# Keys contracted with x instead of with values, and wv applied to the result, in a linear-attention and gated-MLP kernel

## The chip, the core and the metric

The kernel runs on one NeuronCore of a Trainium2 chip. The core has five engines that work side by side, each with its own in-order queue: TensorE (PE, matrix products; loading of the stationary operand is shown as PEld), VectorE (DVE), ScalarE (ACT), GpSimd (POOL) and SyncE (SP, which here only issues DMA transfers). They meet in SBUF, the on-chip memory of 128 partitions, and in the PSUM banks into which TensorE accumulates. The metric is the time in microseconds from the first to the last instruction of one execution, lower is better; a run's time is measured without a profile, and one further execution is profiled.

## What is computed

With S = 2048 rows, D = 1024 columns, H = 32 heads of 32 and F = 3584, all in float32:

```python
def phi(t): return where(t > 0, t + 1, exp(t)) + 1e-6
xn = layernorm(x)
q, k, v = split(xn @ wqkv)                       # each [H, S, 32]
pq, pk = phi(q), phi(k)
kv = einsum("hsd,hse->hde", pk, v)               # 32 x 32 per head, over all rows
z  = einsum("hsd->hd", pk)
o  = einsum("hqd,hde->hqe", pq, kv) / (einsum("hqd,hd->hq", pq, z) + 1e-6)
s  = o @ wo
g  = silu((silu(xn @ w1) * (xn @ w3)) @ w2)
out = x + s * g
```

The attention has no softmax over pairs of rows: keys and values meet only in `kv`, a sum over all rows. Since v = xn wv, the same sum can be taken as kv = wv' (xn' pk), with ' for the transpose, one block of heads at a time.

## The kernel before

**Products.** Float32 operands are split by `split` (L84) into a high part (an ACT copy to the reduced type fp32r) and a low part (a DVE subtraction), and `mm3` (L93) adds three products: high by high, high by low, low by high. All large products are done with seven block products in place of eight, by sums of blocks (the names A11, S1 to S4 on the side of x, B11, T1 to T4 on the side of the weights). `gemm` (L400) is one such product: 256 output columns for 1024 rows, 7 x 4 x 3 = 84 instructions of 512 columns. Its results come as four tiles (n, c): n is the block of 128 output columns, c the block of 512 rows; `use(n, c, tile)` is called on each as it is complete.

**Two halves.** `half(h)` (L525) handles 1024 rows. In half 0, x is loaded, normalised, turned and combined by `prepare_first` and `prepare_rest` (L167, L191), where POOL makes the sums of untransposed blocks (L202 to L205). The first four gemms of half 0 are `early`: they begin on A11 and A12 while the sums are still being made. Then come the keys and values of the four pairs (a pair is 256 columns), the queries (4 gemms) and the two hidden layers (28 gemms). For half 1, `prepare_next` (L211) makes the same operands during half 0 and keeps them in DRAM (`a_d`), from which half 1 loads them at its beginning.

**Keys and values.** `keys_values` (L484) keeps phi(k) of a pair (`pk`), then takes the values; each of the four blocks is turned, key and value, into rows by TensorE transposes against an identity and an ACT eviction (`to_rows`, L477), and a kv step (L509) contracts the rows over 512 tokens, 4 x [128 x 128 x 128] in plain float32, and adds them to `kvacc` in SBUF (L515). These steps are put into `later`.

**What fills the gaps.** `catch_up` (L388) is called six times in an ordinary gemm. It takes one entry of `later`, or else one step of the current job: `next_work` in half 0 (the operands of half 1, then sums of w2 blocks), `attention_work` in half 1 (`spread_z`, denominators, `merge_wo`, which multiplies kv into wo, and `divide`, which scales the queries). Jobs load two ahead into three `job` buffers. What is left over at the end of a half is emitted after its last gemm (L594).

**Buffers and queues.** The `raw` tag has two buffers of 1 MB: x at the beginning, then each weight pair (`Operands.ask`, L297), later the merged wo. The `b` tag of pool `pb` has eight buffers for split operands. SP issues loads in order and waits at each for its buffer; POOL issues most stores in order among its own arithmetic. A planner orders each engine's queue ahead of the run, by readiness in its own model of time and by the order in the program.

Of the kernel before, what the change touches and what calls it, by code (L numbers as in the profile page):

```python
# [22 lines left out]
def tile_linear_attention_times_swiglu(  # L23
# [85 lines left out]
    kvacc = st.tile([P, ND, P], F32, tag="kvacc", bufs=1, name="kvacc")  # L109
    nc.vector.memset(kvacc, 0.0)  # L110

    def small(name):
        return pc.tile([P, C], F32, tag="c", name=name)
# [50 lines left out]
    def operand_tiles(h):  # L164
        return {n: pa.tile([P, 2, ND // 2, C], FR, tag=n, name=f"{n}_{h}") for n in AOPS}

    def prepare_first(A, mom):  # L167

        xs = []
        for g in range(TH // 4):  # L170
            t = load_rows([(2 * g + e) * P for e in range(2)], f"xa{g}")
            xs += [t[:, e] for e in range(2)]
            for i in (2 * g, 2 * g + 1):
                moments(xs[i:i + 1], mom[:, i:i + 1])
                normalise(xs[i], mom[:, i])
                turn_into(A, {"A11": xs[i][:, :C]}, i, f"0_{i}")
# [14 lines left out]
    def prepare_rest(A, mom, i, t0, seconds, behind):  # L191

        with ExitStack() as order:
            for mark in behind:
                order.enter_context(tc.issue_after(mark.ins))
            if i % 2 == 0:
                seconds += load_second(mom, i // 2)
            t1, s1 = seconds[i], small(f"S1x{i}")
            normalise(t1, mom[:, TH // 2 + i])

            a11, a12, a21, a22 = t0[:, :C], t0[:, C:], t1[:, :C], t1[:, C:]
            nc.gpsimd.tensor_add(out=s1, in0=a21, in1=a22)  # L202
            nc.gpsimd.tensor_sub(out=a21, in0=a11, in1=a21)
            nc.gpsimd.tensor_sub(out=a11, in0=s1, in1=a11)
            last = nc.gpsimd.tensor_sub(out=a12, in0=a12, in1=a11)  # L205
        behind.append(last)
        yield
        turned, _ = turn_into(A, {"S2": a11, "S3": a21, "S1": s1, "A22": a22, "S4": a12}, i, f"0_{i}")
        yield turned

    def prepare_next(i):  # L211
# [8 lines left out]
        def steps(_):  # L220
# [22 lines left out]
                yield True  # L243

            a11, a12, a21, a22 = (t[c][:, n * C:(n + 1) * C] for c in range(2) for n in range(2))
            p_ = turn("A11", a11)
            keep("A11", p_)
            nc.scalar.copy(out=a11, in_=p_)
# [232 lines left out]
            nc.tensor.transpose(p_[:, t * P:(t + 1) * P], src[:, t * P:(t + 1) * P], ident)  # L481
        nc.scalar.activation(dst, p_.rearrange("p (t d) -> p t d", t=C // P), AF.Identity, bias=bias)

    def keys_values(h, pair):  # L484

        pk, todo, rows = {}, [], {}

        def use_k(n, c, src):
            j = 2 * pair + n
            pk[n, c] = signed(f"pk{h}_{j}_{c}")  # L490
            z = st.tile([P, 1], F32, tag="z", name="z")
            phi(src, pk[n, c], z)
# [3 lines left out]
        def use_v(n, c, src):  # L496
            if (n, c) == (0, 0):
                v = small(f"v{h}_{pair}")
                nc.scalar.copy(out=v, in_=src)
                src = v  # L500
            todo.append((n, c, src))

        def turn(n, c, v):
            name = f"{h}_{2 * pair + n}_{c}"
            rows[n, c] = pb.tile([P, 2, C // P, P], F32, tag="b", name=f"kvr{name}")
            to_rows(rows[n, c][:, 0], pk[n, c], f"k{name}", 1e-6)
            to_rows(rows[n, c][:, 1], v, f"v{name}")

        def kv(n, c):  # L509
            j = 2 * pair + n  # L510
            r = rows[n, c]
            acc = bank(f"kv{h}_{j}_{c}")[:, :P]
            for t in range(C // P):
                nc.tensor.matmul(acc, lhsT=r[:, 1, t], rhs=r[:, 0, t], start=t == 0, stop=t == C // P - 1)  # L514
            nc.vector.tensor_add(out=kvacc[:, j], in0=acc, in1=kvacc[:, j])  # L515

        def step(i):
            if i:
                kv(*todo[i - 1][:2])
            if i < len(todo):  # L520
                turn(*todo[i])

        return use_k, use_v, [lambda i=i: step(i) for i in range(5)]

    def half(h):  # L525
        A = operand_tiles(h)

        def keys(pair, **how):
            return gemm(ops[f"k{h}_{pair}_"], A, uses[pair][0], **how)

        def values(pair, **how):
            return gemm(ops[f"v{h}_{pair}_"], A, uses[pair][1], **how)

        def run(g):
            for _ in g:
                pass
# [2 lines left out]
            for _ in zip_longest(*gemms):  # L539
                pass  # L540

        uses = [keys_values(h, pair) for pair in range(ND // 2)]
# [23 lines left out]
        for pair in range(ND // 2):  # L566
            if h == 0 and pair < 2:
                run(m[2 * pair])
                run(m[2 * pair + 1])
            elif h and pair == 0:  # L570
                side_by_side(keys(pair, paired=True), values(pair, paired=True))
            else:
                run(keys(pair))
                run(values(pair))
            later.extend(uses[pair][2])
        jobs.append((attention_work(), False) if h else (next_work(), True))
        for pair in range(ND // 2):

# [161 lines left out]
    def divide(m, k):  # L740
# [25 lines left out]

        return Job(load, steps)

    def merge_wo(k):

        both = []
# [7 lines left out]
        def steps(e, t):  # L779
            both.append(t)  # L780
            j = k + e * (ND // 2)
            f = small(f"kvf{j}")[:, :P]
            nc.vector.tensor_mul(f, hmask, kvacc[:, j])
            kvm = st.tile([P, 2, P], FR, tag="kvm", bufs=1, name=f"kvm{j}")
            split(kvm, f)
# [41 lines left out]

    groups = []
    for h in range(NH):
        some = [Operands(wqkv, part * D + pair * 2 * P, f"{'qkv'[part]}{h}_{pair}_", h == 0 and part and pair < 2,  # L830
                         h and part == 2 and pair == 0)
                for parts in ((1, 2), (0,)) for pair in range(ND // 2) for part in parts]
# [6 lines left out]
    for o, o.next in zip(ops, ops[1:]):  # L839
        pass  # L840
    ops = {o.name: o for o in ops}
    stages = in_turn(groups)
    for h in range(NH):
        half(h)
    jobs.append((late_work(), True))
# [300 lines left out]
```

## Time and profile before

| | |
|---|---|
| median of three runs | 2376.68 us (2375.96 to 2380.29) |
| span of the profiled execution | 2378.6 us |
| DMA | 416.77 MB, 175 GB/s on average |
| float32 kv contractions | 128 (256 records) |
| transposes of key rows | 128 |
| transposes of value rows | 128 |

The page of a profile gives each engine's busy time and its share of the span, the same in 40 slices of 59.5 us (a digit is a tenth), and groups of instructions with their count, busy time, mean duration and the idle time before them with what ended it ("<-"). A row of a timeline gives start, duration, engine, line, operation and operands ("out<-in"), and in brackets the idle time before it. Durations of neighbouring products overlap, since the array is pipelined: the price of one is the distance between starts. In a list of waits stand the waiting engine and tile, who ended the wait, and the us in total, the count and the longest.

### The profile page before, as it was taken

To read this page: it belongs to the slowest core of one execution; us is meant where nothing else is said; L and a number is where in the kernel's file an instruction comes from. 1 tells how busy PE (TensorE), PEld (TensorE's weight loads), DVE (VectorE), ACT (ScalarE), POOL (GpSimd) and SP (SyncE) were. 2 spreads that over 40 slices of the span, in tenths; PEclk is the share of its full clock that TensorE was granted. 3 is DMA by queue.
4 is the path that set the end of the run, shared out by engine and by line. 5 is a ranking of instruction groups with operands and counts; after the bars stand their busy time and mean duration, and the time that the engine had idled before them with its cause. 6 is when DMAs were issued, how large, how long until landed. Compare 5 with 4: busy or idle time off the path is not lost.

```text
span 2378.6 us, 30952 instructions
## 1 busy us (share of the span) xinstructions
PE 2330.0 (98%) x10624; PEld 1920.7 (81%) x10624; DVE 1752.6 (74%) x2810; ACT 912.6 (38%) x1621; POOL 637.5 (27%) x752
## 2 busy tenths in 40 slices
PE   6999999999999999999999999999999999999998
PEld 5788888778888888877888887788787788888877
DVE  8755888888887665657788877787755676767698
ACT  4434554342333234434443232324323543343433
POOL 3000122438786420001343434242321000000033
PEclk9999999999999999999999999999999999999999
DMA  3211454567666671125546556464776665766588
GB/s 124 89 53 54 142 169 155 177 184 234 197 221 203 200 280 53 54 76 169 166 158 212 180 173 200 153 191 156 258 230 196 192 205 158 237 194 193 181 277 265
DMA packets 319903, 416.77 MB, mean 175 GB/s; under 512 B 21265, under 2 KB 251665, under 8 KB 319633
## 3 DMA queue, kind: packets, MB, share of 16 engines
q1 hardware_dynamic: 291712, 327.74, 43.6%
q0 software_dynamic: 28032, 87.06, 11.3%
q8 instruction: 83, 1.36, 0.2%
q14 instruction: 76, 0.61, 0.1%
HBM read 277.35 MB, written 141.03 MB: 176 GB/s over the span
## 4 chain that ended last, share of the span: by engine, by line
PE 51%; DMA 4%; issue 4%; DVE 3%; POOL 1%; ACT 1%; SPq 0%; POOLq 0%; DVEq 0%; ACTq 0%
PE cB L96 1%; PE dB L98 1%; PE cB L98 1%; PE dB L96 1%; PE dB L97 1%; PE cB L97 1%; PE aB L98 1%; PE aB L97 1%; PE aB L96 1%; PE bB L98 1%; PE bB L97 1%; PE bB L96 1%; PE kv L514 1%; DVE acc L896 1%; DMA rA22B<-h_d 1%
## 5 line engine op out<-in xcount | busy, mean ns | idle before, releaser
L625 POOL DMA_DIRECT2D h_d<-sg x112 | 82.8, 740 | 334.3 <-DVE sg L621 318.6
L583 POOL DMA_DIRECT2D pq_d<-pq x32 | 17.5, 548 | 469.2 <-DVE pq L475 454.4
L913 POOL DMA_DIRECT2D u_d<-uB x32 | 17.3, 542 | 407.1 <-DVE uB L896 393.0
L896 DVE TENSOR_TENSOR acc<-cB,acc 128x512 f32<-128x512 f32 x50 | 34.4, 687 | 40.6 <-PE cB L98 40.6
L896 DVE TENSOR_TENSOR acc<-dB,acc 128x512 f32<-128x512 f32 x56 | 38.5, 688 | 31.0 <-PE dB L98 31.0
L607 POOL TENSOR_TENSOR hs<-sg 128x256 f32<-128x256 f32 x56 | 60.9, 1087 | 0.0
L605 POOL TENSOR_TENSOR hs<-hs,sg 128x256 f32<-128x256 f32 x56 | 59.9, 1069 | 0.0
L608 POOL TENSOR_TENSOR hs<-sg,hs 128x256 f32<-128x256 f32 x56 | 58.0, 1036 | 1.5
L762 POOL DMA_DIRECT2D qs_d<-qd x32 | 18.0, 561 | 138.8 <-DVE qd L758 138.6
L604 POOL TENSOR_TENSOR hs<-sg,sg 128x256 f32<-128x256 f32 x56 | 49.7, 887 | 1.2
L633 POOL DMA_DIRECT2D h_d<-hs x60 | 46.0, 767 | 4.5 <-POOL hs L608 2.7
L640 POOL TENSOR_TENSOR w<-w 128x256 f32<-128x256 f32 x28 | 26.8, 957 | 55.2 <-DMA w<-in_B_w 47.8
L88 ACT CAST XS4B<-rS4B 128x384 fp32r<-128x384 f32 (+1 forms) x40 | 19.7, 493 | 57.0 <-PE cB L98 40.7
L1027 POOL DMA_DIRECT2D s_d<-s x32 | 17.5, 546 | 87.4 <-DVE s L896 42.4
L763 POOL DMA_DIRECT2D qs_d<-qd x32 | 27.0, 844 | 37.6 <-DVE qd L608 21.7
L88 ACT CAST XA22B<-rA22B 128x384 fp32r<-128x384 f32 (+1 forms) x40 | 19.7, 493 | 44.2 <-PE aB L98 26.4
L88 ACT CAST XA11B<-rA11B 128x384 fp32r<-128x384 f32 (+1 forms) x40 | 19.7, 493 | 43.6 <-PE dB L98 26.8
L96 PE MATMUL cB<-T,XS3B 128*128 128x512 f32 x87 | 34.4, 395 | 2.0 <-ACT XS3B L88 2.0
L88 ACT CAST XS3B<-rS3B 128x384 fp32r<-128x384 f32 (+1 forms) x40 | 19.7, 492 | 43.1 <-PE bB L98 20.4
L96 PE MATMUL aB<-B,XA11B 128*128 128x512 f32 x87 | 34.3, 395 | 1.4 <-ACT XA11B L88 1.4
L514 PEld LDWEIGHTS kv<-kvr 128*128 128x128 f32 x256 | 33.5, 191 | 2.5
L88 ACT CAST XA12B<-rA12B 128x384 fp32r<-128x384 f32 (+1 forms) x40 | 19.7, 494 | 41.0 <-PE dB L98 24.3
(5845 smaller groups left out, 8612.6 us busy)
## 6 DMA issues: line engine op xcount, KB each, us to landing
h_d<-hs POOLq DMA_DIRECT2D x60, 256.0 KB, 3.1
h_d<-sg POOLq DMA_DIRECT2D x56, 256.0 KB, 3.3
w<-in_B_w SPq DMA_DIRECT2D x56, 256.0 KB
wt_d<-w SPq DMA_DIRECT2D x28, 512.0 KB
h_d<-hs SPq DMA_DIRECT2D x52, 256.0 KB
qs_d<-qd POOLq DMA_DIRECT2D x32, 384.0 KB, 3.8
pq_d<-pq POOLq DMA_DIRECT2D x32, 256.0 KB, 3.3
a_dS<-xo SPq DMA_DIRECT2D x16, 512.0 KB
```

The costliest lines, as they stand in the source:

```text
L88: nc.scalar.copy(out=hi, in_=src)
L96: nc.tensor.matmul(acc, lhsT=wh, rhs=ah, start=start, stop=False, skip_group_check=True)
L97: nc.tensor.matmul(acc, lhsT=wh, rhs=al, start=False, stop=False, skip_group_check=True)
L98: nc.tensor.matmul(acc, lhsT=wl, rhs=ah, start=False, stop=stop, skip_group_check=True)
L514: nc.tensor.matmul(acc, lhsT=r[:, 1, t], rhs=r[:, 0, t], start=t == 0, stop=t == C // P - 1)
L604: e.tensor_add(out=s1, in0=a21, in1=a22)
L605: e.tensor_sub(out=s2, in0=s1, in1=a11)
L607: e.tensor_sub(out=s3, in0=a11, in1=a21)
L608: e.tensor_sub(out=s4, in0=a12, in1=s2)
L625: nc.gpsimd.dma_start(out=h_d[i][2 * h + c][:, 2 * n:4 * n + 2, k], in_=src)
L633: queue.dma_start(out=h_d[i][2 * h + c][:, 6 + 4 * e:10 + 4 * e, k], in_=o[e].rearrange("p (e s) -> p e s", s=P))
L896: return V.tensor_add(out=c, in0=src, in1=c)
```

## The change

The value gemms, the turning of the values, the kv steps and `kvacc` are gone. In their place:

- The normalised rows of x and the seven sums of their blocks are stored to DRAM (`x_d`), in half 0 from `prepare_first` and `prepare_rest`, in half 1 from `prepare_next`, all from POOL's queue. `prepare_next` makes four more POOL sums for it per block of rows.
- The key rows, and the sums of them that the seven products need, are stored to `y_d`, also from POOL's queue. All four early gemms of half 0 are now keys.
- After the keys of half 1, `row_products` runs seven products over all rows: each has four steps (two halves, two steps in each; a step is two token blocks of 128 and 24 matrix products), which load x rows and key rows from DRAM through the two `raw` buffers, split them, and accumulate x' pk into four banks. The seventh also loads a block that POOL subtracts. `row_sums` combines the results into `g_d`.
- In half 1's jobs, `key_values(j)` loads the columns of x' pk of block j and the columns of wv, contracts them in float32 (eight products of 128 x 128 x 128 for each of eight blocks), masks the result by head and hands it to `merge_wo`.
- The list of weight operands loses the value parts, and the query operands of half 1 are asked for near the end of `row_products`.

```diff
+    XS = ["A11", "A12", "S1", "S3", "A22", "S2", "S4"]
+    YS = ["Y00", "Y01", "Y10", "R5", "R2", "R4"]
+    x_d = [dram.tile([P, TH // 2, len(XS), C], F32, name=f"x_d{h}") for h in range(NH)]
+    y_d = [dram.tile([P, TH // 2, len(YS), ND // 2, P], F32, name=f"y_d{h}") for h in range(NH)]
+    g_d = [dram.tile([P, ND // 2, C], F32, name=f"g_d{n}") for n in range(4)]
...
+    def keep_rows(h, i, n, t):
+        e, k = XS.index(n), t.shape[1] // C
+        nc.gpsimd.dma_start(out=x_d[h][:, i, e:e + k], in_=t.rearrange("p (n c) -> p n c", c=C))
...
             last = nc.gpsimd.tensor_sub(out=a12, in0=a12, in1=a11)
+            for n, t in (("S1", s1), ("S3", t1), ("S2", t0)):
+                keep_rows(0, i, n, t)
...
+            later.append(lambda: turn(n, c, pk))
...
+            to_rows(t.rearrange("p (t d) -> p t d", d=P), pk, f"k{h}_{pair}_{n}{c}", 1e-6)
+            if (c, n) != (1, 1):
+                keep_keys(h, pair, f"Y{c}{n}", t)
...
+    def row_products():
...
+        ks = [(h, t) for h in range(NH) for t in range(0, TH // 2, 2)]
+        steps = [(i, *k) for i in range(len(ROWS)) for k in ks]
...
+            nc.sync.dma_start(out=raw[:, :2], in_=x_d[h][:, t:t + 2, XS.index(x_)])
+            rows(raw[:, 2:], y_)
+            other = None
+            if less:
+                other = job_tile([P, 2, C], f"yy{i}_{h}{t}")
+                rows(other, less)
...
+            if other is not None:
+                nc.gpsimd.tensor_sub(out=raw[:, 2:], in0=raw[:, 2:], in1=other)
...
+                    o = pb.tile([P, 2, C], FR, tag="b", name=f"xy{n}_{i}_{h}{t + e}")
+                    split(o, raw[:, 2 * n + e])
...
+        data = {s: load(*s) for s in steps[:2]}
+        split_ = {steps[0]: ready(*steps[0])}
...
+            if at + 2 < len(steps):
+                data[steps[at + 2]] = load(*steps[at + 2])
+            if at + 1 < len(steps):
+                split_[steps[at + 1]] = ready(*steps[at + 1])
+            if at + 2 == len(steps):
+                ops["q1_0_"].ask()
+                stages = in_turn(groups[after_rows:])
...
+                    mm3(b[m], (x_[:, 0, c], x_[:, 1, c]), (y_[:, 0], y_[:, 1]),
+                        begins and e == 0 and not onto, ends and e == 1)
...
+    ROWS = [("A22", "Y10", None), ("A12", "Y00", None), ("S2", "R2", None), ("S1", "R4", None),
+            ("S3", "R5", None), ("S4", "Y01", None), ("A11", "R2", "Y00")]
...
-            m = [f(pair, early=True, own=pair == 0 and f is keys) for pair in range(2) for f in (keys, values)]
+            m = [keys(pair, early=True, own=pair == 0) for pair in range(ND // 2)]
...
+            side_by_side(keys(0, paired=True), keys(1, paired=True))
+            for pair in range(2, ND // 2):
                 run(keys(pair))
+            for _ in row_products():
+                pass
...
+            t = job_tile([P, 2, ND // 2, P], f"gw{j}_{e}")
+            nc.sync.dma_start(out=t[:, 0], in_=g_d[2 * e + j % 2][:, :, j // 2 * P:(j // 2 + 1) * P])
...
+            for k in range(ND // 2):
+                nc.tensor.matmul(acc[0], lhsT=t[:, 1, k], rhs=t[:, 0, k], start=e + k == 0, stop=bool(e) and k == ND // 2 - 1)
...
-        work += [j for k in range(ND // 2) for j in merge_wo(k)]
+        for k in range(ND // 2):
+            for e, j in enumerate(merge_wo(k)):
+                work += key_values(k + e * (ND // 2)) + [j]
```

More of the change, by code (lines that the diff above doesn't have):

```diff
@@ L503, in turn @@
[L503 to L523, printed above, removed]
+            later.append(lambda: turn(n, c, pk))
+        def turn(n, c, pk):
+            if (c, n) == (0, 0):
+                t = rows[c, n] = small(f"y00_{h}_{pair}")
+            else:
+                if (1 - c, 1) not in pairs:
+                    pairs[1 - c, 1] = pb.tile([P, 2, C], F32, tag="b", name=f"y{c}_{h}_{pair}")
+                t = rows[c, n] = pairs[1 - c, 1][:, n if c else 0]
+            to_rows(t.rearrange("p (t d) -> p t d", d=P), pk, f"k{h}_{pair}_{n}{c}", 1e-6)
+            if (c, n) != (1, 1):
+                keep_keys(h, pair, f"Y{c}{n}", t)
+            if len(rows) == 4:
+                later.append(sums)
@@ L528, in keys @@
         def keys(pair, **how):
-            return gemm(ops[f"k{h}_{pair}_"], A, uses[pair][0], **how)
-        def values(pair, **how):
-            return gemm(ops[f"v{h}_{pair}_"], A, uses[pair][1], **how)
+            return gemm(ops[f"k{h}_{pair}_"], A, uses[pair], **how)
         def run(g):
@@ L540, in side_by_side @@
                 pass
-        uses = [keys_values(h, pair) for pair in range(ND // 2)]
+        uses = [key_rows(h, pair) for pair in range(ND // 2)]
         if h == 0:
@@ L565, in half @@
                     nc.sync.dma_start(out=A[n][:, :, k].bitcast(F32), in_=a_d[n][:, :, k])
[L566 to L572, printed above, removed]
+        if h == 0:
+            for g in m:
+                run(g)
+        else:
+            side_by_side(keys(0, paired=True), keys(1, paired=True))
+            for pair in range(2, ND // 2):
                 run(keys(pair))
-                run(values(pair))
-            later.extend(uses[pair][2])
+            for _ in row_products():
+                pass
         jobs.append((attention_work(), False) if h else (next_work(), True))
@@ L767, in divide, with key_values, load, steps @@
         return Job(load, steps)
+    kvf = {}
+    def key_values(j):
+        acc = []
+        def load(e):
+            t = job_tile([P, 2, ND // 2, P], f"gw{j}_{e}")
+            nc.sync.dma_start(out=t[:, 0], in_=g_d[2 * e + j % 2][:, :, j // 2 * P:(j // 2 + 1) * P])
+            rows = wqkv[e * C:(e + 1) * C, 2 * D + j * P:2 * D + (j + 1) * P]
+            nc.sync.dma_start(out=t[:, 1], in_=rows.rearrange("(k p) n -> p k n", p=P))
+            return t
+        def steps(e, t):
+            yield True
+            if not acc:
+                acc.append(bank(f"kv{j}")[:, :P])
+            for k in range(ND // 2):
+                nc.tensor.matmul(acc[0], lhsT=t[:, 1, k], rhs=t[:, 0, k], start=e + k == 0, stop=bool(e) and k == ND // 2 - 1)
+            if e:
+                kvf[j] = st.tile([P, P], F32, tag="kvf", bufs=1, name=f"kvf{j}")
+                nc.vector.tensor_mul(kvf[j], acc[0], hmask)
+            yield True
+        return [Job(lambda e=e: load(e), lambda t, e=e: steps(e, t)) for e in range(2)]
     def merge_wo(k):
@@ L781, in steps @@
             j = k + e * (ND // 2)
[L782 to L783 removed]
             kvm = st.tile([P, 2, P], FR, tag="kvm", bufs=1, name=f"kvm{j}")
[L785 removed]
+            split(kvm, kvf[j])
             o = []
@@ L829, in tile_linear_attention_times_swiglu @@
     for h in range(NH):
-        some = [Operands(wqkv, part * D + pair * 2 * P, f"{'qkv'[part]}{h}_{pair}_", h == 0 and part and pair < 2,
-                         h and part == 2 and pair == 0)
-                for parts in ((1, 2), (0,)) for pair in range(ND // 2) for part in parts]
+        some = [Operands(wqkv, part * D + pair * 2 * P, f"{'qk'[part]}{h}_{pair}_", h == 0 and part == 1,
+                         h and part == 1 and pair == 1)
+                for part in (1, 0) for pair in range(ND // 2)]
         some += [Operands((w1, w3)[e], pair * 2 * P, f"{'gu'[e]}{h}_{pair}_", second=h == 0 and e and pair == NF // 2 - 1)
@@ L841, in tile_linear_attention_times_swiglu @@
     ops = {o.name: o for o in ops}
-    stages = in_turn(groups)
+    after_rows = [ops["q1_0_"] in g for g in groups].index(True)
+    ops["k1_3_"].next = None
+    stages = in_turn(groups[:after_rows])
     for h in range(NH):
```

103 lines of the change are left out of this document (90 added, 13 removed).

## The prediction

> **What bounds the kernel now.** I read the page's busy shares and slices first, then the list of what TensorE waited for, then stretches of the timeline.
>
> ```profile
> span 2378.6 us, 30952 instructions
> PE 2330.0 (98%) x10624; PEld 1920.7 (81%) x10624; DVE 1752.6 (74%) x2810; ACT 912.6 (38%) x1621; POOL 637.5 (27%) x752
> PE   6999999999999999999999999999999999999998
> PE tA L160 <- DVE v L144: 11.5, 1, 11.5
> PE tS L160 <- POOL xa L204: 5.0, 4, 3.5
> PE bv__823 L96 <- ACT T2v__726 L88: 3.4, 1, 3.4
> 180.00:240.00 60.00, 60.00 (x324) 51.66 (x323) 31.23 (x60) 26.23 (x46) 1.16 (x2) 1.00 0.16 54
> 860.00:1050.00 190.00, 189.31 (x966) 161.03 (x964) 110.40 (x209) 83.12 (x143) 2.53 (x5) 1.00 0.22 74
> ```
>
> PE is busy 98% of the span; of its 48.6 idle us the three waits shown, all in the first slices, are 20. The last two rows are windows (us, then busy PE, PEld, DVE, ACT, POOL, granted clock, DMA share, GB/s) over key, value and query products: PE without a gap, at full clock, DVE near 55%, DMA a fifth used. So there a PE instruction removed is time removed, and one added is time added, until something starves PE. The windows have products with and without the key/value steps between them, and PE is full in both: those steps do not cover another engine's lateness.
>
> **What it removes.** The unit prices come from PE's timeline, as differences of start times, since the records overlap.
>
> ```profile
> 140.08 0.39 PE L98 MATMUL ck__1230<-S,T3k__1055 128*128 128x512 f32 x1
> 140.30 1.05 PE L514 MATMUL kv<-kvr 128*128 128x128 f32 x8
> 141.19 0.60 PE L481 MATMUL trk<-ident,pk 128*128 128x128 f32 x4
> 141.63 0.60 PE L481 MATMUL trv<-ident,c21v__1172 128*128 128x128 f32 x4
> 141.99 0.48 PE L96 MATMUL dk__1231<-S,T1k__1117 128*128 128x512 f32 x1
> 142.30 0.40 PE L97 MATMUL dk__1231<-S,T1k__1117 128*128 128x512 f32 x1
> 144.58 0.39 PE L98 MATMUL dk__1231<-S,T1k__1117 128*128 128x512 f32 x1
> 249.72 0.39 PE L97 MATMUL cq__2147<-S,T3q__1917 128*128 128x512 f32 x1
> 267.62 0.39 PE L98 MATMUL bq__2310<-S,T2q__2163 128*128 128x512 f32 x1
> L514 PE MATMUL kv<-kvr 128*128 128x128 f32 x256 | 33.7, 274 | 0.0
> L482 ACT ACTIVATE kvr<-trv 128x512 f32<-128x512 f32 x32 | 19.0, 593 | 0.0
> ```
>
> From 142.30 to 144.58 are ten gaps between products of 512 columns, 0.228 us each; the last two timeline rows are the first and the last of 80 in a row, 17.90 / 79 = 0.2266. The four contractions of one kv step (eight records) take 141.19 - 140.30 = 0.89 us, the four transposes of a block 141.63 - 141.19 = 0.44. There are 256 / 8 = 32 kv steps and 32 evictions of turned values. All go: 32 x (0.89 + 0.44) = **-42.6 us** of PE. Key rows are still turned, 32 times as before.
>
> **What takes their place.** The eight value gemms are 8 x 84 products of 512 columns. The row products are seven, each contracted over 1024 rows (8 blocks of 128), for 4 bands of 128 x columns, by 3 products for the split: 7 x 8 x 4 x 3 = 672, the same 672. So **0**. Applying wv afterwards is 8 blocks x 8 contractions of 128 x 128: sixteen groups of four, of the same form as kv, 16 x 0.89 = **+14.2 us**. PE alone: **-28.4**. DVE, ACT and POOL work does not decide this as long as it is in time; 88 weight-tile operations on DVE go, 112 splits come.
>
> **Can the row stream feed PE?** This is the largest unknown: before, a product's right side lay in SBUF; now every operand comes back from DRAM. A step is two token blocks: 24 products, 24 x 0.2266 = 5.44 us, and needs 1.05 MB (two loads of 512 KB), that is 193 GB/s; the last of the seven also loads the subtrahend, 1.57 MB or 289 GB/s. The nearest case is where the merged wo comes back through the same two "raw" buffers, is split and freed.
>
> ```profile
> 1656.34 20.17 SPq L1088 DMA_DIRECT2D wpr<-wp_d  x10
> 1660.00:1670.00 10.00, 10.00 (x46) 8.29 (x45) 9.54 (x16) 6.51 (x13) 1.48 (x2) 1.00 0.82 274
> 1669.42 2.40 ACT L88 CAST wp<-wpr 128x512 fp32r<-128x512 f32 x4 [2.54 <-DMA wpr<-wp_d]
> L89 DVE TENSOR_TENSOR wp<-wpr,wp 128x512 fp32r<-128x512 f32 x28 | 22.1, 835 | 1.6 <-ACT wp L88 1.6
> 58.48 0.37 SPq L300 DMA_DIRECT2D wv__719<-in_A_wqkv  x1
> 65.50 0.69 DVE L320 TENSOR_TENSOR wv__719<-wv__719 128x512 f32<-128x512 f32 x1 [3.12 <-DMA wv__719<-in_A_wqkv]
> ```
>
> Ten 512 KB loads were issued in 20 us with other loads between, at 274 GB/s and an 0.82 DMA share: 193 fits. A lone 1.05 MB load (58.48 to 65.50) takes 7.0 us, four splits about 0.8 x 4 = 3.3. Count from the start of a step n. Its tile slots come free half at 2.72, half at 5.44, and step n+2 is split into them, done near 7.5. Then that raw buffer is free and step n+4 is loaded into it; it must be split by 4 x 5.44 = 21.8, its first half from 19.8. That leaves 12.3 us for a load of 7: 5 to spare, so the six ordinary products should run at PE's pace: **0**, between 0 and the first rival. At the beginning, the last pair's key rows must be turned, stored and loaded again before the third step, 10.9 us in: half a product, phi, transposes, eviction and store come to about 6 us, load and split to 5: **+1** (0 to 2). In the last product, 4 x (1.57 / 0.274 - 5.44) = 1.2 us, the first query weights (another 1.05 MB, 3.8 us at that rate) partly on top, and a POOL subtraction of 1024 columns in front of the splits: **+2** (0 to 6).
>
> The Trainium skill (DMA: Bandwidth & Descriptors, Bandwidth) puts the limit of one core's HBM traffic at about 358 GB/s. By that the 289 GB/s of the last product would fit and its 1.2 us would be nothing; the rows quoted here reach 274 and do not show which is right.
>
> **The start gets longer.** The x rows and their sums are now stored from POOL's queue, in program order between its additions.
>
> ```profile
> 37.59 1.61 POOL L205 TENSOR_TENSOR xa<-xa 128x512 f32<-128x512 f32 x1
> 39.16 1.28 POOL L202 TENSOR_TENSOR S1x<-xb 128x512 f32<-128x512 f32 x1
> 54.56 1.27 POOL L205 TENSOR_TENSOR xa<-xa 128x512 f32<-128x512 f32 x1
> 54.53 1.12 PE L160 MATMUL tS<-ident,xa 128*128 128x128 f32 x4 [3.54 <-POOL xa L204]
> 66.69 0.39 PE L98 MATMUL ck__704<-S,T3k__693 128*128 128x512 f32 x1
> 70.50 0.50 PE L96 MATMUL bv__823<-S,T2v__726 128*128 128x512 f32 x1 [3.42 <-ACT T2v__726 L88]
> 71.31 0.63 PE L97 MATMUL ck__704<-A,T4k__697 128*128 128x512 f32 x1
> 74.30 0.57 PE L98 MATMUL ck__704<-A,T4k__697 128*128 128x512 f32 x1
> L583 POOL DMA_DIRECT2D pq_d<-pq x32 | 17.5, 548 | 469.2 <-DVE pq L475 454.4
> pq_d<-pq POOLq DMA_DIRECT2D x32, 256.0 KB, 3.3
> ```
>
> POOL's additions run without a gap between blocks (37.59 + 1.61 meets 39.16), and PE already waits for the fourth block: POOL is the chain here. Three blocks' stores, 9 x 0.55 us, stand ahead of the fourth block's last sum: **+4.9** (0, if they are queued behind all sums, to 4.9). Second, the raw buffer that x occupied is released only when the store of the last sum has landed: three more issues (1.6) and 3.3 to land after POOL's end, against transposes ending some 2.6 after it: the second gemm's weights, for which PE already waits from 66.69 to 70.50, come **+2.3** later still (0 to 2.3). The four early stores have POOL to themselves (its first addition is at 32.67 in the same timeline), but share the DMA queues with weights: 0 to 2, I take 0.
>
> After that 3.4 us gap eight products run 0.43 us apart (71.31 to 74.30) before the pace returns. The Trainium skill (TensorE: Matmul & The Clock Gate, Part 1) has the array fall to half rate after an idle window of about 3.4 us and recover after as long a busy one; the trace agrees, 0.43 against 0.228. By that rule each new long gap would cost another 1.6 us; mine lengthen two gaps that are long already, so the sum stays.
>
> **The ends of the halves.** In half 0, six more job steps for each of four row blocks (24) fill the 32 gemms x 6 places that were 168 of 192 used; the few left over are weight sums needed much later: 0. In half 1 the 32 steps of the wv blocks turn 169 of 192 into 201: two divisions of queries spill past the last gemm and keep the three job buffers in which the attention's first operands are loaded.
>
> ```profile
> 1608.40 0.81 SPq L985 DMA_DIRECT2D r2q<-qs_d  x2
> 1654.57 0.61 ACT L88 CAST XS3s<-r2q 128x512 fp32r<-128x512 f32 x1
> 1662.16 0.39 PE L96 MATMUL B11s<-wp,XA11s 128*128 128x512 f32 x1
> ```
>
> Those loads now lie 46 us ahead of their use (1608.40 to 1654.57), which covers most of a 9-step delay (9 x 2.72 = 24 us) and more: **+1.5** (0 to 8, the latter if all four loads and the splits come after the last gemm).
>
> **Sum.** -42.6 + 14.2 + 1 + 2 + 4.9 + 2.3 + 1.5 = -16.7. The profiled execution's span is 2378.6, 1.9 above the median of the runs: 2376.7 - 16.7 = **2360 us**. With every unknown at its low end the change is -28.4 (2348), with every one at its high end -28.4 + 2 + 6 + 7.2 + 2 + 8 = -3.2 (2373.5).
>
> **Rivals.** *The row stream starves PE* (slower). If the two loads in flight do not overlap, each step lasts as long as its load: 24 x (7.0 - 5.44) + 4 x (10.5 - 5.44) = 57.7, and 2360 + 57.7 - 3 = 2415; it becomes slower than before from 17 us of waiting, a mean step of 6.05 us, or 173 GB/s. For it: every operand passes DRAM, buffers and two splits, and the lone load is 7.0 us long. Against it: 274 GB/s in the row above. Chance 0.17. If such gaps gathered to 3.4 us, the clock rule of the Trainium skill named above would add 1.6 us to each. *The start hides it*: POOL's stores are queued after the sums and the release is not late; then -16.7 - 7.2, 2353. For it: only the order of POOL's queue decides; against: the stores come earlier in the program. Chance 0.13. *The gain is eaten* by several terms near their high ends and half of the attention spill, or the wv contractions waiting for their loads at the head of PE's queue (1 us at each of 16 groups is 16): around 2376, no difference. Against the latter: the denominators before take their loads with the same lookahead, and their stretch after 1050 us has no place in PE's list of waits. Chance 0.09. Forecast (2351 to 2371): 0.58; 0.03 stays for what I did not think of.
>
> **The numbers.** Less than 0.2% (4.8 us) cannot be told from no change. Forecast and the hidden start are faster (0.71), the eaten gain is the same (0.10), starvation and half of the unforeseen slower (0.19). The range reaches from all unknowns low with a little more, 2346, into the first half of starvation, 2388; the forecast's own is 2351 to 2371.
>
> **What would show it.** No trv group, and kv in 128 records of the same 0.89-us groups. In the row products 24 products per 5.44 us with PE full and 190 GB/s in the window; a PE wait for splits there, or a mean step over 6 us, is the starvation. PE's wait for POOL before the fourth block near 5 us in place of 3.5, with POOL's store issues between sums. Job loads of r0q to r6q at most a few us before the attention's first product. I am wrong if PE's idle time grows by more than 28 us, or if its busy time falls by less than 25.

## The result and the profile after

The changed kernel takes 2399.34 us (median of four runs, 2395.23 to 2399.72), the kernel before 2378.48 beside it (2375.96 to 2384.16): a ratio of 1.0079, 95% interval 1.0063 to 1.0095. It is slower by 19 us or so, where 2360 and "faster" were forecast; the time lies outside the range.

The page of the changed kernel, its span, busy shares, TensorE's slices and the group that applies wv:

```profile
span 2397.6 us, 30961 instructions
PE 2315.7 (97%) x10368; PEld 1896.1 (79%) x10368; DVE 1772.2 (74%) x2781; ACT 919.6 (38%) x1639; POOL 751.0 (31%) x892
PE   6999999999999889999999899999999999999998
L902 PE MATMUL kv<-gw 128*128 128x128 f32 x128 | 16.8, 274 | 0.0
```

256 PE records are gone as expected, but PE is busy only 14.3 us less, and idle 2397.6 - 2315.7 = 81.9 us against 48.6, which is 33.3 more. The forecast had named both as signs of being wrong: busy time down by less than 25 us, idle time up by more than 28. What TensorE waited for, in the changed kernel (us in total, count, longest):

```profile
PE trk L505 <- DVE pk L499: 11.7, 4, 6.7
PE tA L162 <- DVE v L146: 11.5, 1, 11.5
PE tS L162 <- POOL xa L212: 6.4, 3, 4.2
PE cg__11115 L101 <- DVE c22g__11150 L462: 6.2, 1, 6.2
PE B11s L101 <- ACT XA11s L93: 3.7, 1, 3.7
PE dg__2322 L101 <- DVE c22g__2353 L468: 2.6, 1, 2.6
PE g L101 <- ACT xy L93: 2.3, 1, 2.3
PE bk__6485 L101 <- ACT T2k__6324 L93: 2.0, 1, 2.0
```

The first, fourth, fifth and last of these were in none of the forecast's terms at such a size. To place them, the span is cut at the first starts of products in PE's timeline. The forecast's column is its own terms put into these stretches: each half loses four value gemms (4 x 84 x 0.2266 = 76.1) and sixteen kv steps with turned values (21.3).

| stretch, us | before | after | difference | forecast |
|---|---|---|---|---|
| to the first hidden gemm of half 0 | 297.0 | 206.5 | -90.5 | -97.4 + 7.2 = -90.2 |
| to the last hidden gemm of half 0 | 516.0 | 510.9 | -5.1 | 0 |
| to the first key gemm of half 1 | 35.4 | 35.4 | 0 | 0 |
| to the first hidden gemm of half 1 (keys, row products, queries) | 266.6 | 348.5 | +81.9 | -97.4 + 152.3 + 3 + 1.8 = +59.7 |
| to the last hidden gemm of half 1 | 533.6 | 554.8 | +21.2 | +12.4 |
| to the second product group of the attention (as) | 38.1 | 50.2 | +12.1 | +1.5 |
| to the output layer (B11B) | 140.6 | 136.3 | -4.3 | 0 |
| to the end | 551.3 | 555.1 | +3.8 | 0 |

(1.8 and 12.4 are the two and the fourteen of the sixteen wv groups that fall into those stretches.) The start came out to the microsecond. Three stretches are too long, by 22, 9 and 11 us, and they hold the four waits. The last row stays open: in the experiments below, none of which edits it, it lies between 553.6 and 558.4, also with the kernel before as the base (e7, 555.3).

**The first of the three: PE waits to turn the last keys.** A timeline of the changed kernel at the end of half 1's keys:

```profile
847.46 0.69 DVE L491 TENSOR_TENSOR c12k__7136<-dk__7002,uk__6978 128x512 f32<-128x512 f32 x1 [0.94 <-PE dk__7002 L103]
848.39 3.72 ACT L93 CAST xy<-xy 128x512 fp32r<-128x512 f32 x7
849.03 4.30 DVE L94 TENSOR_TENSOR xy<-xy,xy 128x512 fp32r<-128x512 f32 x7 [0.88 <-ACT xy L93]
852.50 0.62 ACT L497 ACTIVATE pk<-c21k__7109 128x512 f32<-128x512 f32 x1
854.19 0.69 DVE L499 SCALAR_TENSOR_TENSOR pk<-c21k__7109,pk 128x512 f32<-128x512 f32 x1 [0.86 <-ACT pk L498]
854.95 1.12 PE L505 MATMUL trk<-ident,pk 128*128 128x128 f32 x4 [6.66 <-DVE pk L499]
```

The last key blocks are complete at 848. ACT and DVE then make seven splits for the row products, and only behind them (852.50) phi of the keys. The transposes that wait for phi stand at the head of PE's queue, and the row products, whose splits are finished, stand behind them. Before, a key block was turned together with the value block of its place, so that the value gemm lay between its phi and its transposes; now its transposes go into the list as soon as phi is issued, and behind the last pair there is no gemm left.

**The second and third: divisions hold DVE, and the attention's operands are loaded late.** From DVE's, PE's and SP's timelines of the changed kernel, with the row of its list of waits for such divisions:

```profile
DVE qd L873 <- DMA qd<-pq_d: 42.4, 9, 7.9
1363.97 0.69 DVE L873 SCALAR_TENSOR_TENSOR qd<-qd 128x512 f32<-128x512 f32 x1 [7.58 <-DMA qd<-pq_d]
1374.01 0.80 PE L101 MATMUL cg__11115<-A,T4g__11153 128*128 128x512 f32 x1 [6.24 <-DVE c22g__11150 L462]
1670.11 0.80 SPq L1128 DMA_DIRECT2D r0q<-qs_d  x2
1673.49 0.53 PE L101 MATMUL B11s<-wp,XA11s 128*128 128x512 f32 x1 [3.69 <-ACT XA11s L93]
```

With 201 steps for 192 places the attention's first operand (r0q) is loaded at 1670.11, 3.4 us ahead of the product that needs it. Before, it was 70 us: the product stood at 1662.16, and r0q in SP's timeline of the kernel before at

```profile
1592.51 0.85 SPq L985 DMA_DIRECT2D r0q<-qs_d  x2
```

And a division whose query block has not landed holds DVE, 7.58 us here, with the sums of a hidden gemm behind it. DVE waits 42.4 us in this way, 5.2 us in the kernel before.

**The row stream is fed.** Windows of the changed kernel over row products, the last two of them in the seventh (columns as before):

```profile
950.00:960.00 10.00, 10.00 (x46) 8.29 (x45) 4.31 (x8) 4.46 (x8) 0.00 (x0) 1.00 0.65 208
990.00:1000.00 10.00, 10.00 (x45) 8.19 (x45) 5.73 (x10) 1.85 (x5) 4.57 (x5) 1.00 0.91 301
1000.00:1010.00 10.00, 7.67 (x30) 5.92 (x29) 4.50 (x8) 3.36 (x6) 2.35 (x1) 0.91 0.83 277
```

PE is full at 208 GB/s and even at 301; one wait of 2.33 us in the last product, for a split, is nearly all that PE idles there.

### The profile page after: what moved, and what is told of

Read it like the earlier page. It is cut to its first block, busy times and chain, and to the rows that moved or that the text cites. A ratio compares the mean times of both kernels' runs of the same rounds, so it can differ in the third digit from the quotient of the medians.

```text
span 2397.6 us, 30961 instructions
## 1 busy us (share of the span) xinstructions
PE 2315.7 (97%) x10368; PEld 1896.1 (79%) x10368; DVE 1772.2 (74%) x2781; ACT 919.6 (38%) x1639; POOL 751.0 (31%) x892
## 4 chain that ended last, share of the span: by engine, by line
PE 43%; issue 10%; DMA 7%; DVE 4%; POOL 3%; ACT 1%; SPq 0%; POOLq 0%; DVEq 0%; ACTq 0%
PE g L101 2%; PE g L102 2%; PE g L103 2%; DMA qd<-pq_d 1%; PE cB L101 1%; PE cB L103 1%; PE cB L102 1%; PE aB L101 1%; PE aB L102 1%; PE dB L101 1%; PE aB L103 1%; PE dB L103 1%; PE dB L102 1%; DMA qs_d<-qd 1%; DMA rA22B<-h_d 1%
## 5 line engine op out<-in xcount | busy, mean ns | idle before, releaser
L94 DVE TENSOR_TENSOR xy<-xy,xy 128x512 fp32r<-128x512 f32 x112 | 75.9, 720 | 69.5 <-ACT xy L93 69.2
L93 ACT CAST xy<-xy 128x512 fp32r<-128x512 f32 x112 | 63.9, 620 | 86.2 <-PE g L103 60.1
L102 PE MATMUL g<-xy,xy 128*128 128x512 f32 x224 | 88.5, 395 | 0.0
L103 PE MATMUL g<-xy,xy 128*128 128x512 f32 x224 | 88.1, 394 | 0.0
L101 PE MATMUL g<-xy,xy 128*128 128x512 f32 x224 | 83.0, 395 | 2.8 <-ACT xy L93 2.3
L509 POOL DMA_DIRECT2D y_d<-y x40 | 29.7, 751 | 102.5 <-ACT y L506 79.7
L877 POOL DMA_DIRECT2D qs_d<-qd x32 | 17.9, 560 | 132.2 <-DVE qd L873 122.2
L873 DVE SCALAR_TENSOR_TENSOR qd<-qd 128x512 f32<-128x512 f32 x32 | 21.9, 684 | 42.4 <-DMA qd<-pq_d 42.4
L101 PEld LDWEIGHTS g<-xy,xy 128*128 128x128 f32 x224 | 42.2, 189 | 12.5 <-ACT xy L93 2.9
L102 PEld LDWEIGHTS g<-xy,xy 128*128 128x128 f32 x224 | 42.9, 192 | 9.0
L103 PEld LDWEIGHTS g<-xy,xy 128*128 128x128 f32 x224 | 42.9, 192 | 9.0
```

Source lines behind the costliest of these rows:

```text
L93: nc.scalar.copy(out=hi, in_=src)
L94: return nc.vector.tensor_sub(out=lo, in0=src, in1=hi.bitcast(F32))
L101: nc.tensor.matmul(acc, lhsT=wh, rhs=ah, start=start, stop=False, skip_group_check=True)
L102: nc.tensor.matmul(acc, lhsT=wh, rhs=al, start=False, stop=False, skip_group_check=True)
L103: nc.tensor.matmul(acc, lhsT=wl, rhs=ah, start=False, stop=stop, skip_group_check=True)
```

## The experiments

Two theories stood against each other for the middle of the kernel: that the key blocks are turned too early (theory A), and that the job list does not fit its places (theory B); a third, that the x-sum stores at the start and the subtrahend of the last product cost what the forecast said, concerned terms that had been forecast. Each ratio is to the kernel before, run beside it.

**e1: turn keys later.** In half 1 the turning of a key block is held back by two blocks, and the first query gemm runs ahead of the row products, so that PE has work while the last keys are finished.

```diff
-            later.append(lambda: turn(n, c, pk))
+            held.append(lambda: turn(n, c, pk))
+            if len(held) > 2 * h:
+                later.append(held.pop(0))
...
+            later.extend(held)
+            held.clear()
+            query(0)
             for _ in row_products():
```

> Two edits to the changed kernel: in half 1 a key block is turned two blocks after its phi instead of at once, and one query gemm of half 1 runs between the keys and the row products, so that the last pair's rows are stored in time. Theory: TensorE's 11.7 us of waits for phi before the transposes, the 6.7 us at the beginning of the row products among them, and the half-rate stretches after them are what the half-1 keys lose; then the waits for phi vanish and the time falls by 13 to 16 us, to about 2385. Rival: the keys' loss comes from operands that are late (DMA and weight splits at the start of the half); then the waits only change their name and the time falls by less than 4 us.

2398.8 us, ratio 1.008 (1.0063 to 1.0097): no gain in the sum, a miss, with two large effects inside. The stretch of keys, row products and queries fell from 348.5 to 332.8 us, and the waits of trk are gone. The attention's start rose from 50.2 to 71.2: the moved query gemm takes six places away, 201 steps for 186. Theory A has its 15.7 us, and theory B takes them back.

**e2: make the jobs fit half 1.** Each of the 24 divisions takes one place less; nothing else differs from the changed kernel.

```diff
         def steps(t):
-            for _ in range(3):
+            for _ in range(2):
                 yield True
```

> One edit to the changed kernel: a division of queries takes three places between products instead of four, so that the jobs of half 1 need 177 of the 192 places instead of 201. Theory: the overrun delays the attention's first loads by some 60 us and costs the 12 us between the last gemm and the attention, and the divisions' late loads cost up to 6 us before; then the stretch from the last gemm's start to the attention shrinks from 50 to 38 us and the time falls by 12 to 18 us, to about 2384. Rival: the attention starts late because its weights come late through the raw buffers, whatever the divisions do; then less than 4 us.

2378.35 us, ratio 0.9992 (0.9982 to 1.0001). The hidden gemms of half 1 fall from 554.8 to 544.4, the attention's start from 50.2 to 38.1, which is what it was before. In the list of what TensorE waited for neither cg__11115 nor B11s is left, and r0q is again loaded 50 us ahead (its row in SP's timeline):

```profile
1606.26 0.80 SPq L1128 DMA_DIRECT2D r0q<-qs_d  x2
```

So the edit is worth about 21 us, the whole loss against the kernel before. Of these, 12.1 lie at the attention's start, where the next stretch takes 5.2 back (141.5 in place of 136.3), and 10.4 in the hidden gemms. But the edit does two things: it ends the overrun, and it makes every division shorter. DVE's waits at L873 are gone too, and this run does not say by which of the two.

**e5: both.** The edits of e1 and e2 together.

> The edits of the first two experiments together: key blocks turned two blocks later in half 1, one query gemm ahead of the row products, divisions with three places. Theory: the first edit gained 15.7 us between half 1's first gemm and its first hidden gemm and lost more at the attention's start, because the query gemm that it moved took six places from the jobs (15 steps over instead of 9); with divisions of three places 177 steps fit the 186 places, so both gains stand: 2399 - 16 - 21 = about 2362, faster than before the change. Rival: the stretch before the attention is now too short for the divisions' chain of loads and stores whatever their count; then about 2378.

2368.3 us, ratio 0.9951 (0.9934 to 0.9967): faster than the kernel before, and 31 us below the changed kernel. The stretches are 331.5, 547.4 and 38.1: both gains stand in their places, as theories A and B demand when their causes are separate. In the whole time they do not add in full: the second edit took 16.3 us from its own stretch and 10 from the time of e2, since the hidden gemms are 3 us longer and the other stretches another 4.

**e6: the query first and the jobs that fit, but keys turned at once.** e5 without the `held` list, to part the two edits of e1.

> As the kernel with both edits, but key blocks are turned at once, as in the change; only the query gemm stands ahead of the row products, and divisions have three places. Theory: turning at once makes TensorE wait for phi in every pair, so of the 15.7 us only the last pair's wait (6.7 us and its half-rate stretch, about 8) is gained: about 2370, with the waits of 2 us before transposes still in the list. Rival: what helped was the query gemm alone; then about 2362.

2378.74 us, ratio 0.9995 (0.9985 to 1.0006). What TensorE waited for, in e6:

```profile
PE trk L505 <- DVE pk L499: 9.1, 4, 4.1
```

Keys to queries take 342.5 us against 331.5 in e5 and 347.8 in e2: 11 us belong to the turning at once and 5 to having a gemm in front of the row products. In the whole time e6 is no better than e2 and misses the 2370 that was expected, since its hidden gemms are 3 us and its start 2 us longer. No edit touches the start here, but the planner orders the queues of every kernel anew: starts that were not edited lie between 205.3 and 212.0 us in these runs.

**e7: the kernel before, with 32 idle places.** Sixteen jobs that do nothing, of two places each, stand among its merges of wo; the sum is again 201.

```diff
+        def idle(_):
+            yield True
+            yield True
...
+                work += [Job(lambda: None, idle), Job(lambda: None, idle), j]
```

> One edit to the kernel before the change: sixteen empty jobs of two places each among the merging of wo, so that half 1's jobs need 201 of 192 places, with no load and no product added. Theory: the overrun alone costs what the change loses there, 12 us before the attention and some 6 to 10 us in the hidden gemms: 2379 + 20 = about 2399. Rival: the loss comes from the wv blocks' own loads and contractions; then within 3 us of before.

2406.29 us, ratio 1.0111 (1.0094 to 1.0127). What TensorE waited for, in e7:

```profile
PE B11s L96 <- ACT XA11s L88: 24.7, 1, 24.7
```

The attention's start takes 74.4 us in place of 38.1, the hidden gemms 529.0 in place of 533.6. No operand, product or transfer was added: places alone make the kernel before some 26 us slower. They do it at the attention's start and not in the hidden gemms. DVE's waits for query blocks are 17.7 us in total here, all of them behind 1650 us, when the last hidden gemm has begun; in the changed kernel five of the nine, 24 us, stand between 1340 and 1480. The overrun alone thus gives the late start, but not what the changed kernel loses in its hidden gemms.

**e3: make the jobs fit half 0.** Three steps without work between two sums are dropped from each of the four row blocks of `prepare_next`.

```diff
-            for _ in range(3):
-                yield True
```

> One edit to the changed kernel: the preparation of half 1's operands takes three places fewer for each block of rows, so that the jobs of half 0 need 180 places instead of 192. Theory: the sums of w2 that spill past the last gemm hold SP's queue, so that half 1's operands are loaded some 8 us late against its first gemm, and TensorE waits 3 us and then runs 12 products at half rate; then the time falls by 5 to 7 us, to about 2393. Rival: half 1 starts with the same gap as before the change whatever the jobs do; then no difference.

2413.82 us, ratio 1.0145 (1.013 to 1.016), a miss. Keys to queries fell by 2 us only; the start, which the edit does not touch, rose by 5.5, and the hidden gemms of half 0 by 9.6, with waits of 1 to 3 us for the sums c22 between 205 and 480 us, such as these in e3's list of groups over that window:

```profile
L101 PE MATMUL cq__1853<-A,T4q__1762 128*128 128x512 f32 x4 | 2.3, 571 | 3.1 <-DVE c22q__1887 L460 3.1
L101 PE MATMUL cg__2974<-A,T4g__2887 128*128 128x512 f32 x4 | 2.2, 538 | 2.1 <-DVE c22g__3008 L460 2.1
```

So the places without work seem to keep the preparation from crowding DVE. What the overrun of half 0 costs was left open by this.

**e4: the x-sum stores after all sums.** The twelve stores of the start are issued behind POOL's last addition.

```diff
-            for n, t in (("S1", s1), ("S3", t1), ("S2", t0)):
-                keep_rows(0, i, n, t)
+            stores = [(0, i, n, t) for n, t in (("S1", s1), ("S3", t1), ("S2", t0))]
...
+        if len(sums_made) == TH // 2:
+            with tc.issue_after(last.ins):
```

> One edit to the changed kernel: in half 0 the twelve stores of the sums of x stand behind all of POOL's sums instead of between them. Theory: the stores between the sums make the fourth block 4.9 us late and the first hidden gemm of half 0 starts 5 us earlier without them, though the second gemm's weights wait longer for the released x buffer: between 0 and 5 us gained in the end, about 2396. Rival: the start is set by VectorE and the transposes; then the fourth block comes no earlier and the time stays.

2409.93 us, ratio 1.0127 (1.0112 to 1.0142), a miss. From e4's timeline of PE:

```profile
53.55 0.66 PE L162 MATMUL tS<-ident,xa 128*128 128x128 f32 x4 [2.40 <-POOL xa L214]
78.31 0.79 PE L101 MATMUL bk__733<-S,T2k__719 128*128 128x512 f32 x1 [21.22 <-ACT T2k__719 L93]
```

The fourth block came 3.7 us earlier (57.27 in the changed kernel), so the stores between the sums do cost that. But the buffers of x are then released behind twelve stores: the next weights (wk__712) are loaded at 64.13 in place of 50.00, and PE waits 21 us.

**e8: the best version, with both terms removed.** e5, with the x-sum stores issued from SP's queue, and the difference of the last product made once and stored in place of a subtrahend loaded beside it.

```diff
-        nc.gpsimd.dma_start(out=x_d[h][:, i, e:e + k], in_=t.rearrange("p (n c) -> p n c", c=C))
+        queue.dma_start(out=x_d[h][:, i, e:e + k], in_=t.rearrange("p (n c) -> p n c", c=C))
...
-                keep_rows(0, i, n, t)
+                keep_rows(0, i, n, t, nc.sync)
...
+            nc.gpsimd.tensor_sub(out=rows[0, 0], in0=r2, in1=rows[0, 0])
+            keep_keys(h, pair, "R6", rows[0, 0])
...
-            ("S3", "R5", None), ("S4", "Y01", None), ("A11", "R2", "Y00")]
+            ("S3", "R5", None), ("S4", "Y01", None), ("A11", "R6", None)]
```

> As the kernel with both edits, and two more edits far apart in time: half 0 stores the sums of x from SP's queue instead of POOL's, and the seventh row product reads a stored difference instead of loading a subtrahend that POOL subtracts. Theory: without POOL's twelve issues half 0's first hidden gemm starts 5 us earlier (202 us instead of 207), and the row products lose their wait of 1 to 2 us and the half-rate stretch after it (152 to 153 us instead of 155 to 159): about 8 us below the kernel with both edits. Rivals: the start is held by VectorE, then 0 there; the last product waits for the next weights rather than for the subtrahend, then 0 there.

2367.04 us, ratio 0.9945 (0.9928 to 0.9962), the fastest of all, though not to be told from e5 by the runs, where 8 us were expected. The start is 5.7 us shorter (200.2 against 205.9), but the stretches behind it are together 1.7 longer. The row products are no shorter (154.5 against 154.7): the wait in the last product is gone, but one of 2.12 us for an eviction of their results stands elsewhere in the same stretch, in e8's timeline of PE:

```profile
881.45 0.50 PE L101 MATMUL g<-xy,xy 128*128 128x512 f32 x1 [2.12 <-ACT gu L631]
```

**e9: short weight jobs in half 0.** e8, with one step less in each sum of w2 blocks, to settle what e3 left open.

```diff
             nc.sync.dma_start(out=wt_d[u][:, :, cols], in_=t)
-            yield True
```

> On top of e8, the 56 sums of w2 blocks in half 0 (two halves of 28) take two job places each in place of three; the operands of half 1 are prepared as before, so nothing is added to the catch-ups of the first hidden gemms. Theory (what was left over of half 0's jobs, weight sums and their stores, stands in the load queue ahead of the first operands of half 1, and the 3.0 us of waits with the half-rate stretch at 752 to 766 us of e8 come from it): no job is left at the boundary, the loads of A are issued before the first key gemm, both waits (1.92 and 1.13) vanish, first key gemm to first hidden gemm of half 1 falls from 332.8 to 327 to 329, and the time to 2361 to 2364 (ratio to before 0.992 to 0.993). Rival (the waits belong to half 1's first gemm itself, whose operands are made from tiles freed only by the last gemm of half 0): no job left over, but the waits stay, 332 to 333 and 2366 to 2368. Second rival (faster jobs crowd DVE during the hidden gemms, as in e3): waits for DVE c22 appear between 205 and 480 us, and half 0 gets longer by 3 us or more.

2368.35 us, ratio 0.9958 (0.9943 to 0.9973): no change against e8. Both the theory and the second rival are in it. Keys to queries fell from 332.8 to 326.1; the hidden gemms of half 0 rose from 509.0 to 516.3, with waits for the sums c22 of 0.7 to 2.3 us, which stand between 588 and 670 us, later than the rival had them. How SP stood at the boundary, in the changed kernel:

```profile
740.97 4.91 SPq L776 DMA_DIRECT2D wt_d<-w  x1
...
754.38 11.12 SPq L681 DMA_DIRECT2D A<-a_dA  x8
```

The last loads of A are issued at 754.38, when the first key gemm has begun (752.8). In e8 they stand at 745.65, 1 us behind it (744.6); in e9 at 746.60, 5 us ahead of it (751.7). The work that is left over at the boundary is work that half 0 then does not hold: 7 us there, 7 us here.

## Why the prediction was wrong

**PE's arithmetic held.** kv steps and turned values went; the wv groups have 128 records, and one of them lasts 0.81 us from its start to the next product's (1110.11 to 1110.92 in PE's timeline) against the 0.89 that was taken, and no group had PE wait (0.0 in its row above). In e5 and e8, where the new waits are mostly gone, PE's busy time is 25.0 and 26.0 us below that of the kernel before, against -28.4.

**The start held.** Forecast +7.2, measured +6.9. The division into 4.9 and 2.3 is less sure: PE waited 4.2 us for the fourth block where near 5 was forecast, and it came 2.7 us later than before (57.27 against 54.53) and 3.7 later than in e4. e8 moves the stores off POOL's queue and gains 5.7, where 4.9 was the stores' term. The order of release, the other term, shows in e4, where a later release cost 21 us of waiting.

**The row stream held.** The rival of starvation did not happen: PE is full in the windows, 158.8 us for the row products against 152.3 + 3. The last product's +2 was one wait of 2.33 us and the slower products behind it. The Trainium skill (DMA: Bandwidth & Descriptors, Bandwidth) has about 358 GB/s as the limit, against which the forecast set 274; the trace agrees that the last product's 289 fits: 301 GB/s over a window of it. It does not agree on the limit: a window at the end of this document has 371 GB/s.

**The step that failed first: half 1's job overrun, +1.5 (0 to 8).** The attention's start took 12.1 us more than before, and the next stretch gave 4.3 back; e7 shows the same overrun, alone, at 36.3 and 7.3. The forecast set 46 us of lead against nine places of 2.72 us, 24 us. But the first operand to be loaded is r0q and not r2q, and the attention's loads stand in the program behind the steps that are left after the last gemm, while the last divisions hold the job buffers. Counted from the start of the last hidden gemm, r0q was loaded 56 us ahead of it before and 14 us behind it now: the overrun cost 70 us of lead and not 24. That the upper end, all four loads after the last gemm, was priced at 8 us was the mistake of size: e7 shows 24.7 us of waiting for that case. The rival of the eaten gain had the spill too, at half of that price.

**The second: "Key rows are still turned, 32 times as before."** The number is right, 128 transposes and the same price; the place was not looked at. The forecast said that the kv steps did not cover another engine's lateness, from windows with PE full. Removed with them were the value gemms between keys and transposes, and these did: each transpose needs phi, three operations on ACT and DVE, and behind the last pair these engines now have the splits of the row products in front. Turning at once costs 11 us (e6 against e5), the missing gemm in front of the row products 5 more (e2 against e6). The forecast had the chain, about 6 us, and set it against the third step's load, not against the transposes at the head of PE's queue: +1 (0 to 2).

**In no term: divisions that hold DVE.** The hidden gemms of half 1 are 9 us longer than forecast, and in them stand five waits of DVE for query blocks and PE's wait of cg__11115. DVE's five are gone in e2 (544.4 us in place of 554.8) and absent in e7, which has the overrun but not the wv blocks. So shorter divisions cure them; that the overrun causes them is not shown, and what does stays open. A changed kernel with the same divisions and fewer places elsewhere would tell.

**Half 0's overrun, 0:** right in the sum for a reason that the forecast did not have. It gives 7 us at the boundary and takes 7 from half 0 (e9).

In whole times, the edit of e2 gives back 21 us and that of e1 on top of it another 10 (e5), where the forecast had 1.5 and 1 for what they mend. With these in its sum, -16.7 becomes +12; the profiled spans differ by +19.0. The 7 us between are not placed. Part of them may be what the moved query gemm costs elsewhere: in its own stretch the edit of e1 gains 16 and not 10, and the hidden gemms are 3 us longer in e5 and in e6, which both move it.

## What to carry to other kernels

Count the places of every list of background work before and after a change, and price an overrun by what is then emitted last and who needs it first, and not by the number of steps. When work is taken out between a producer and an in-order consumer, ask what the removed work covered: a full engine in the profile does not show that its order has slack. Undo the costs one at a time and together: here one repair alone showed no gain, the other a tie with the kernel before, and both made a kernel that beats it.

## What the runs showed of the hardware

Waits of about the same length were followed by different rates. From PE's timeline of the changed kernel, and two of its windows, where the third number from the end is the granted clock:

```profile
263.95 0.67 PE L101 MATMUL dg__2322<-S,B22g__2255 128*128 128x512 f32 x1 [2.62 <-DVE c22g__2353 L468]
264.42 0.63 PE L102 MATMUL dg__2322<-S,B22g__2255 128*128 128x512 f32 x1
264.85 0.63 PE L103 MATMUL dg__2322<-S,B22g__2255 128*128 128x512 f32 x1
...
800.64 0.63 PE L505 MATMUL trk<-ident,pk 128*128 128x128 f32 x4 [2.42 <-DVE pk L499]
...
802.31 0.40 PE L102 MATMUL ak__6790<-A,B11k__6582 128*128 128x512 f32 x1
802.54 0.40 PE L103 MATMUL ak__6790<-A,B11k__6582 128*128 128x512 f32 x1
264.00:267.40 3.40, 3.40 (x8) 2.64 (x9) 0.98 (x2) 3.39 (x5) 1.59 (x2) 0.52 0.33 135
801.00:804.00 3.00, 2.68 (x16) 2.10 (x15) 2.74 (x9) 3.00 (x7) 0.00 (x0) 1.00 0.09 29
```

After 2.62 us of idling the products start 0.43 us apart for about 3.4 us (to 267.40), at a granted clock of 0.52; after 2.42 us the first products start 0.23 apart, at 1.00. The wait of 2.33 us at 1007.52 is followed by the slow rate too. A wait can therefore cost more than half as much again as it lasts (eight products at 0.43 in place of 0.23 us, 1.6 us behind 2.62), and whether it does is not settled by its length. The Trainium skill (TensorE: Matmul & The Clock Gate, Part 1) has a free-running window of about 3.4 us behind the clock; a window that runs free would explain the mixture, but a wait of 2.33 us that halves the rate is shorter than the idle window that it states. The slower products count as busy, which is a part of why PE's busy time fell by 14 us and not by 28; how large a part was not counted. Which of the waits meet the window was not tested.

Loads and stores together moved 371 GB/s over 28 us at the boundary of the halves, in the changed kernel's windows (the last number):

```profile
752.00:780.00 28.00, 24.82 (x102) 19.74 (x101) 22.53 (x27) 10.80 (x18) 14.91 (x18) 0.94 1.04 371
```
